# Sums of a masked attention spread over rows: broadcast and f32 transposes against two f32r parts and selector matmuls

## The chip, the cores and the metric

One core of one Trainium2 chip runs the whole program as one launch. The metric is the device time of one execution in microseconds (us); lower is better. TensorE is called PE below (its weight loads PEld), VectorE DVE, ScalarE ACT, GpSimd POOL, and SP is the engine that issues the DMAs.

## The reference, cut to what matters

Eight head pairs of attention (batch 2, 8 heads, 768 tokens, head size 64) with a mask from cluster numbers, and behind it two MLP layers (1536 tokens, 512 to 2048 to 512). Only the division by the sum of the exponentials bears on the change:

```python
    scores = scale * np.matmul(q, k.transpose(0, 1, 3, 2))
    scores = np.where(mask, scores, -1000000000.0)
    scores = scores - np.max(scores, axis=-1, keepdims=True)
    attn = np.exp(scores)
    attn = attn / (np.sum(attn, axis=-1, keepdims=True) + 1e-09)
    return np.matmul(attn, v).astype(np.float32)
```

## The kernel before, in words

The attention goes in 96 units of 128 query rows: 8 pairs (a batch and two heads), 2 heads, 3 groups of 256 rows, 2 tiles of 128. So a pair is 12 units. The kernel writes out the order of every engine's queue by hand (`tc.manual_schedule`, L340), in the loop at L985: in the round of unit u it issues the four score matmuls of u (`scores`, L714), the evacuation of a finished group (`drain`, L789), the exponentials of u-1 (`exps`, L730), the row maxima of u (`maxima`, L725), then the steps that are due in phase E of this round, then six f32 transposes of the exponentials of u-2 (`transposes`, L746), their split into two f32r parts by ACT (`highs`, L763) and DVE (`lows`, L767), then the 12 matmuls per group with the values in two halves (`attend`, L773), and last the steps due in phase L. A step due at a whole number x runs in phase L of round x, one due at x.5 in phase E of the next round (`at_`, L817, and L911).

PSUM is tight: `ps_s` has two tiles for scores, `ps_t` two for the transposes (so `pt` of unit u takes the tiles that DVE's `lows` of u-1 must have read), `ps_o` one for the sums of products, and `ps_m` one single bank, tag "m" (L203). That bank is taken in turn by the centroid dots (`dps`, L521), their transposes (`dt`, L548), the one-hot transposes (`ot`, L612) and the spread of the reciprocals (`rp_`, L861). The steps that prepare a later pair have due times in the table `STEADY` (L24): among them the dots at 5 to 7, `dt=10`, its last reader `dn=12.5` (DVE, L564: it multiplies `dt`), `ot0=20`, `ot1=21`. They count from 24 units ahead of that pair's first unit.

`finish(n)` (L820) divides pair n by its sums, with due times from `FINISH` (pairs 0 to 5), `FINISH_NEXT` (pair 6) and `FINISH_LAST` (pair 7), counted from the unit behind the pair's last one. POOL adds 1e-9 to the sums (`sg`, L835), DVE takes the reciprocals `rs` (128 rows x 6 tiles x 2 heads, L843), ACT copies them in two halves into `rx`, each reciprocal repeated over 64 columns (L851, 128x384 each). PE transposes `rx` by 128x128 pieces, three and three, into `rp_` (`spread`, L863), where a reciprocal then lies along the column of its query, repeated over the 64 rows of its head. DVE multiplies the products `xs` by it (`divide`, L872). Then ACT and POOL split `xs` into the MLP's f32r inputs `xh` and `xl` (L891, L903).

Behind unit 95 the MLP follows; its weights are converted from unit 82 on by ACT, DVE and POOL (`to_float32`, L154) between the attention's instructions.

Of the kernel before, what the change touches and what calls it, by code (L numbers as in the profile page):

```python
# [9 lines left out]
F32 = mybir.dt.float32  # L10
F32R = mybir.dt.float32r
# [3 lines left out]
ALU = mybir.AluOpType  # L15
# [32 lines left out]
]  # L48

FINISH = [3, 4, 7, 11, 14, 15, 16, 17, 19]  # L50
FINISH_NEXT = [3, 4, 5, 6, 7, 8, 9, 10, 14]
FINISH_LAST = [1, 1, 2, 3, 3, 3, 5, 5, 5]

MANUAL = 8
# [1 line left out]
P = 128  # L56
# [4 lines left out]
def kernel(  # L61
# [20 lines left out]
    nc = tc.nc  # L82
    B, NPAIR, _, _, S = qk_dim.shape
    H = 2 * NPAIR
    C = P // H
    D = P // 2
    NF, _, DM = w_out1.shape
    J = S // P
# [4 lines left out]
    HS = S // 2  # L93
# [10 lines left out]
    ident = const.tile([P, P], F32, name="ident")  # L104
    make_identity(nc, ident)
    identr = const.tile([P, P], F32R, name="identr")
# [96 lines left out]
    ps_m = ctx.enter_context(tc.tile_pool(name="ps_m", bufs=1, space=PSUM, reuse_waits="tile"))  # L203
# [114 lines left out]
    with ExitStack() as actx:  # L318
# [4 lines left out]
        ap4 = actx.enter_context(tc.tile_pool(name="ap4", bufs=1))  # L323
# [3 lines left out]
        def warm(n, pool=None):  # L327

            if pool is None:
                wps = ps_t.tile([P, 512], F32, tag="t", name="wps")  # L330
            else:
                wps = pool.tile([P, 2, 512], F32, tag="s", name="wps")[:, 0]
            for _ in range(n):
                nc.tensor.transpose(wps[:, 0:P], ident, ident)
# [71 lines left out]
            nc.vector.tensor_tensor(out=clz[:, :, mid], in0=csrc, in1=chz.bitcast(F32)[:, :, mid], op=ALU.subtract)  # L406

        todo = defaultdict(list)  # L410
        E, L = 0, 1
# [2 lines left out]
        def at(u, phase=L):  # L414
            def register(fn):
                todo[u, phase].append(fn)
            return register
# [7 lines left out]
        halves = [slice(t * HS, (t + 1) * HS) for t in range(2)]  # L425
# [391 lines left out]
        def at_(k):  # L817
            return at(int(-(-k // 1)), L if k % 1 == 0 else E)

        def finish(n):  # L820

            b, i = pairs[n]
            u0 = (n + 1) * UPP
            cuts = [slice(3 * t, 3 * t + 3) for t in range(2)]
            q = {}
            last = n == len(pairs) - 1
            ks = FINISH_LAST if last else FINISH_NEXT if n == len(pairs) - 2 else FINISH

            @at_(u0 + ks[0])
            def _():  # L830
                q["rs"] = ap4.tile([P, J, 2], F32, tag="rs", name="rs")
                q["sg"] = []
                for hh in range(2):
                    sg = ap4.tile([P, J], F32, tag="sg", name="sg", bufs=2)
                    nc.gpsimd.tensor_scalar(  # L835
                        out=sg, in0=sums.pop((n, hh)), scalar1=1e-9, scalar2=None, op0=ALU.add
                    )
                    q["sg"].append(sg)

            @at_(u0 + ks[1])  # L840
            def _():
                for hh in range(2):
                    nc.vector.reciprocal(out=q["rs"][:, :, hh], in_=q["sg"][hh])  # L843

            for t in range(2):

                @at_(u0 + ks[2 + t])
                def _(t=t):
                    if t == 0:
                        q["rx"] = ap4.tile([P, J, 2, D], F32, tag="rx", name="rx")  # L850
                    nc.scalar.copy(  # L851
                        out=q["rx"][:, cuts[t]], in_=q["rs"][:, cuts[t], :, None].to_broadcast([P, 3, 2, D])
                    )

            for t in range(2):

                def spread(t):
                    if last and t == 1:
                        rp_ = ps_t.tile([P, 512], F32, tag="t", name="rp_")
                    else:  # L860
                        rp_ = ps_m.tile([P, 512], F32, tag="m", name="rp_")  # L861
                    for j in range(3):
                        nc.tensor.transpose(  # L863
                            rp_[:, j * P : (j + 1) * P],
                            q["rx"][:, 3 * t + j].rearrange("p h d -> p (h d)"),
                            ident,
                        )
                    q["rp", t] = rp_

                def divide(t):  # L870
                    xs = xs_[n]
                    nc.vector.tensor_tensor(  # L872
                        out=xs[:, halves[t]], in0=xs[:, halves[t]], in1=q["rp", t][:, 0:HS], op=ALU.mult
                    )

                if last:
                    at_(u0 + ks[4 + t])(lambda t=t: spread(t))
                    at_(u0 + 4)(lambda t=t: divide(t))
                else:

                    @at_(u0 + ks[4 + t])
                    def _(t=t):
                        spread(t)
                        divide(t)

            where = slice(b * S, (b + 1) * S)
            for t in range(2):

                @at_(u0 + ks[6 + t])
                def _(t=t):  # L890
                    nc.scalar.copy(out=xh[:, i, where][:, halves[t]], in_=xs_[n][:, halves[t]])  # L891

            @at_(u0 + ks[8])
            def _():
                xs = xs_.pop(n)
                if last:
                    for eng, cut in zip((nc.vector, nc.gpsimd), halves):
                        eng.tensor_tensor(
                            out=xl[:, i, where][:, cut], in0=xs[:, cut],
                            in1=xh.bitcast(F32)[:, i, where][:, cut], op=ALU.subtract,  # L900
                        )
                    return
                nc.gpsimd.tensor_tensor(  # L903
                    out=xl[:, i, where], in0=xs, in1=xh.bitcast(F32)[:, i, where], op=ALU.subtract
                )
# [6 lines left out]
        for n in range(len(pairs)):  # L912
            finish(n)
        for entry in PRELUDE:
# [11 lines left out]
            else:  # L926
                steps[int(n[0])][name]()
        at(1)(lambda: warm(8))
        drains = []
        keys = [(n, hh, g) for n in range(len(pairs)) for hh in range(2) for g in range(NQ)]  # L930

# [17 lines left out]
        for F in range(2):  # L949
            todo[NU - 14, L].append(lambda F=F: begin(F))  # L950
            for j in range(2):
                start = NU - 12 + (0, 3, 6, 9)[2 * F + j]
# [685 lines left out]
```

## Time and profile before

| | us |
|---|---|
| median of 3 runs | 781.37 (781.03 to 781.65) |
| the profiled execution, its time | 782.5 |
| the profiled execution, its span from first to last instruction | 780.7 |
| mean granted TensorE clock in it, as a share of full speed | 0.996 |

A row of the timeline has the start and the length in us, the engine, the line of the kernel, the operation, the tiles it writes and reads, and in brackets the idle time of the engine ahead of it with what ended it; "x6" stands for six instructions merged. The chain of waits gives the work that ended last, followed back from the end: there the pieces of one engine follow each other without a gap, so that a piece's length is the time that its instructions really took on the path.

### The profile page before, as it was taken

How to read it: one execution, taken by the hardware profiler on the slowest of the kernel's cores; microseconds unless marked ns; L12 is line 12 of the kernel's file. 1: busy time of each engine (PE TensorE's matmuls, PEld its weight loads, DVE VectorE, ACT ScalarE, POOL GpSimd, SP SyncE). 2: the span in 40 equal slices, each digit the busy share in tenths (PEclk: the TensorE clock that was granted, in tenths of full speed). 3: DMA queues.
4: the chain of work that ended last, by engine and by line, in shares of the span. 5: the costliest groups of instructions: out<-in, count | busy, mean ns of one | idle time of the engine just before them, and what ended most of it. 6: DMA issues, size and time to landing. Idle time of an engine off the chain costs nothing.

```text
span 780.7 us, 12017 instructions
## 1 busy us (share of the span) xinstructions
PE 760.1 (97%) x4073; PEld 651.5 (83%) x4073; DVE 650.6 (83%) x1015; ACT 552.2 (71%) x1130; POOL 507.9 (65%) x510
## 2 busy tenths in 40 slices
PE   7699999999999899999999999999999999999998
PEld 6598999999999788788888888887888888888887
DVE  6778889889899767489967768799989898998965
ACT  5788999999899878365766766856965555655530
POOL 5666677886643545478758778598785766756810
PEclk9999999999999999999999999999999999999999
DMA  9857467566452350012112121211220302212004
GB/s 248 217 147 194 126 179 183 143 158 163 101 132 81 106 182 34 0 55 82 37 72 81 55 81 60 76 54 33 103 80 29 108 27 81 82 54 82 1 0 162
DMA packets 27101, 75.92 MB, mean 97 GB/s; under 512 B 4480, under 2 KB 7680, under 8 KB 27040
## 3 DMA queue, kind: packets, MB, share of 16 engines
q1 hardware_dynamic: 27040, 75.16, 32.9%
q8 instruction: 32, 0.52, 0.3%
q14 instruction: 29, 0.24, 0.1%
HBM read 49.36 MB, written 3.15 MB: 67 GB/s over the span
## 4 chain that ended last, share of the span: by engine, by line
PE 81%; ACT 6%; POOL 4%; DVE 3%; issue 3%; DMA 2%; SPq 0%; POOLq 0%; ACTq 0%; DVEq 0%
PE acc L1310 26%; PE hp L1146 9%; PE x L1146 8%; PE pt L749 7%; PE o L779 7%; PE v L1146 4%; PE acc L287 4%; PE s L721 4%; PE s L722 4%; PE hp L235 3%; PE z L1146 2%; DMA tok<-in_qk_tok_dram 1%; PE dps L525 1%; POOL sq L470 1%; ACT e L736 1%
## 5 line engine op out<-in xcount | busy, mean ns | idle before, releaser
L727 DVE TENSOR_REDUCE nm<-s 128x1 f32<-128x768 f32 x96 | 91.1, 949 | 17.4 <-PE s L722 17.2
L769 DVE TENSOR_TENSOR pl<-pt,ph 128x384 fp32r<-128x384 f32 x192 | 97.6, 550 | 8.3 <-ACT ph L765 7.6
L765 ACT CAST ph<-pt 128x384 fp32r<-128x384 f32 x192 | 84.1, 488 | 15.4 <-PE pt L749 14.7
L736 ACT ACTIVATE e<-s,nm 128x768 f32<-128x768 f32 x96 | 88.2, 918 | 3.4 <-DVE nm L727 2.9
L749 PE MATMUL pt<-ident,e 128*128 128x128 f32 x576 | 83.6, 278 | 6.0 <-DVE pl L769 6.0
L749 PEld LDWEIGHTS pt<-ident,e 128*128 128x128 f32 x576 | 67.4, 142 | 18.5 <-DVE pl L769 15.0
L1326 DVE TENSOR_TENSOR y<-y,acc 128x512 f32<-128x512 f32 x97 | 65.9, 680 | 15.9 <-PE acc L1310 15.6
L1333 POOL TENSOR_TENSOR y<-y,n 128x512 f32<-128x512 f32 x42 | 57.0, 1362 | 32.2 <-ACT n L1323 32.2
L1310 PE MATMUL acc<-oh,gl 128*128 128x512 f32 x190 | 74.0, 389 | 0.0
L1310 PE MATMUL acc<-oh,gh 128*128 128x512 f32 x190 | 74.0, 389 | 0.0
L1310 PE MATMUL acc<-ol,gh 128*128 128x512 f32 x190 | 74.0, 389 | 0.0
L175 DVE SCALAR_TENSOR_TENSOR r<-raw,r 128x512 uint32<-128x512 uint32 x64 | 65.6, 1025 | 4.0 <-issue 3.1
L721 PE MATMUL s<-ak,aq 128*128 128x384 f32 x192 | 68.9, 359 | 0.0
L722 PE MATMUL s<-mk,mq 80*128 80x384 f32 x192 | 65.7, 342 | 2.5 <-DVE mk L633 2.5
L182 POOL TENSOR_TENSOR tw<-m,r 128x512 uint32<-128x512 uint32 x26 | 34.0, 1308 | 48.4 <-DVE r L175 47.4
L187 POOL TENSOR_TENSOR il<-tw,ih 128x512 fp32r<-128x512 f32 x26 | 34.3, 1320 | 34.0 <-ACT ih L186 34.0
L182 POOL TENSOR_TENSOR t<-m,r 128x512 uint32<-128x512 uint32 x38 | 50.1, 1318 | 9.1 <-DVE r L175 9.1
L187 POOL TENSOR_TENSOR ol<-t,oh 128x512 fp32r<-128x512 f32 x32 | 46.8, 1461 | 11.6 <-ACT oh L186 11.6
L170 DVE TENSOR_SCALAR m<-m 128x512 f32<-128x512 f32 x64 | 47.5, 742 | 3.9 <-ACT m L166 3.8
L1146 PE MATMUL hp<-xl,ih 128*128 128x512 f32 x120 | 46.9, 391 | 1.4 <-DVE xl L1365 1.4
L1310 PE MATMUL acc<-gl,oh 128*128 128x512 f32 x120 | 46.8, 390 | 0.0
L1146 PE MATMUL hp<-xh,il 128*128 128x512 f32 x120 | 46.7, 390 | 0.0
(295 smaller groups left out, 2357.7 us busy)
## 6 DMA issues: line engine op xcount, KB each, us to landing
raw<-in_w_in_dram SPq DMA_DIRECT2D x32, 512.0 KB, 3.2
raw<-in_w_out_dram SPq DMA_DIRECT2D x32, 512.0 KB, 3.3
tok<-in_qk_tok_dram SPq DMA_DIRECT2D x8, 768.0 KB, 6.0
ak<-hi SPq DMA_DIRECT2D x31, 192.0 KB, 3.0
dim<-in_qk_dim_dram SPq DMA_DIRECT2D x6, 768.0 KB, 5.7
aq<-hi SPq DMA_DIRECT2D x16, 192.0 KB, 3.6
aq<-lo SPq DMA_DIRECT2D x16, 192.0 KB, 4.0
rawv<-in_v_dram SPq DMA_DIRECT2D x8, 384.0 KB, 4.0
```

The source lines that it names most:

```text
L182: nc.gpsimd.tensor_tensor(out=t.bitcast(U32), in0=mu, in1=r, op=ALU.add)
L187: nc.gpsimd.tensor_tensor(out=low, in0=t, in1=high.bitcast(F32), op=ALU.subtract)
L721: nc.tensor.matmul(s[:, c, 0:HS], lhsT=aq[:, qs], rhs=ak[:, ks], start=True, stop=False)
L722: nc.tensor.matmul(s[:, c, 0:HS], lhsT=mq[:, qs], rhs=mk[:, ks], start=False, stop=True)
L727: nc.vector.tensor_reduce(out=nm, in_=st[u]["s"][:, :, 0:HS], axis=AX.XY, op=ALU.max, negate=True)
L736: nc.scalar.activation(out=e.rearrange("p (a j) c -> p a (j c)", a=2), in_=st[u]["s"][:, :, 0:HS], func=AF.Exp, bias=st[u]["nm"], scale=1. ...
L749: nc.tensor.transpose(pt[:, j * P : (j + 1) * P], st[u]["e"][:, 3 * a + j, :], ident)
L765: nc.scalar.copy(out=dh, in_=src)
L769: nc.vector.tensor_tensor(out=dl, in0=src, in1=dh.bitcast(F32), op=ALU.subtract)
L1146: nc.tensor.matmul(o, lhsT=x_, rhs=y_, start=start and j == 0 and n == 0, stop=stop and j == len(ah) - 1 and n == 2, skip_group_check=chain,)
L1310: nc.tensor.matmul(acc, lhsT=a_, rhs=b_, start=s_ == 0 and n == 0, stop=s_ == 1 and n == 2)
L1326: nc.vector.tensor_tensor(out=y, in0=y, in1=acc, op=ALU.add)
```

## The change

For pairs 0 to 6 the reciprocals are no longer repeated by ACT and transposed whole. POOL splits `rs` into two f32r parts, 12 columns of high parts and 12 of low ones (`parts`, 128x24). One f32r transpose puts them into the bank of `ps_m` as 24 rows x 128 columns; ACT copies that to `rt`. `spread` then makes each 128x128 piece of `rp_` by a matmul of 24 rows: the stationary operand is a constant `sel`, which is 1 where the row is the high or the low part of the wanted reciprocal, and the moving operand is `rt`. `sel` is made once by POOL in round 11, in the buffer of `rx`. The new due times: `parts` at the due time of the reciprocals plus 0.5, the transpose at 13 and ACT's copy at 13.5 (pair 6: 5 and 5.5), where the two copies of ACT had 7 and 11 (pair 6: 5 and 6). `spread` and `divide` keep theirs (14 and 15; pair 6: 7 and 8). Pair 7 stays as it was.

```diff
--- before.py
+++ after.py
@@ -47,8 +47,8 @@
     "lt 1",
 ]
 
-FINISH = [3, 4, 7, 11, 14, 15, 16, 17, 19]
-FINISH_NEXT = [3, 4, 5, 6, 7, 8, 9, 10, 14]
+FINISH = [3, 4, 13, 13.5, 14, 15, 16, 17, 19]
+FINISH_NEXT = [3, 4, 5, 5.5, 7, 8, 9, 10, 14]
 FINISH_LAST = [1, 1, 2, 3, 3, 3, 5, 5, 5]
 
 MANUAL = 8
@@ -407,6 +407,14 @@
 
 
 
+        sel = ap4.tile([4 * J, 2 * J, D], F32R, tag="rx", name="sel")
+
+        def selectors():
+            both = ap4.tile([4 * J, 2 * J], F32, tag="rs", name="both")
+            eye = ident[0 : 4 * J]
+            nc.gpsimd.tensor_tensor(out=both, in0=eye[:, 0 : 2 * J], in1=eye[:, 2 * J : 4 * J], op=ALU.add)
+            nc.gpsimd.tensor_copy(out=sel, in_=both[:, :, None].to_broadcast([4 * J, 2 * J, D]))
+
         todo = defaultdict(list)
         E, L = 0, 1
         UPP = 2 * J
@@ -842,15 +850,40 @@
                 for hh in range(2):
                     nc.vector.reciprocal(out=q["rs"][:, :, hh], in_=q["sg"][hh])
 
-            for t in range(2):
-
-                @at_(u0 + ks[2 + t])
-                def _(t=t):
-                    if t == 0:
-                        q["rx"] = ap4.tile([P, J, 2, D], F32, tag="rx", name="rx")
-                    nc.scalar.copy(
-                        out=q["rx"][:, cuts[t]], in_=q["rs"][:, cuts[t], :, None].to_broadcast([P, 3, 2, D])
-                    )
+            def rows_of_sums():
+                q["rp"] = {}
+                ps = ps_m.tile([P, 512], F32R, tag="m", name="rt")
+                nc.tensor.transpose(ps[0 : 4 * J, 0:P], q["parts"], identr)
+                q["ps"] = ps
+
+            if last:
+                for t in range(2):
+
+                    @at_(u0 + ks[2 + t])
+                    def _(t=t):
+                        if t == 0:
+                            q["rx"] = ap4.tile([P, J, 2, D], F32, tag="rx", name="rx")
+                            q["rp"] = {}
+                        nc.scalar.copy(
+                            out=q["rx"][:, cuts[t]], in_=q["rs"][:, cuts[t], :, None].to_broadcast([P, 3, 2, D])
+                        )
+
+            else:
+
+                @at_(u0 + ks[1] + 0.5)
+                def _():
+                    q["parts"] = ap4.tile([P, 4 * J], F32R, tag="parts", name="parts")
+                    rs = q["rs"].rearrange("p j h -> p (j h)")
+                    high, low = q["parts"][:, 0 : 2 * J], q["parts"][:, 2 * J : 4 * J]
+                    nc.gpsimd.tensor_copy(out=high, in_=rs)
+                    nc.gpsimd.tensor_tensor(out=low, in0=rs, in1=high.bitcast(F32), op=ALU.subtract)
+
+                at_(u0 + ks[2])(rows_of_sums)
+
+                @at_(u0 + ks[3])
+                def _():
+                    q["rt"] = ap4.tile([4 * J, P], F32R, tag="rt", name="rt")
+                    nc.scalar.copy(out=q["rt"], in_=q["ps"].bitcast(F32)[0 : 4 * J, 0:P])
 
             for t in range(2):
 
@@ -860,17 +893,19 @@
                     else:
                         rp_ = ps_m.tile([P, 512], F32, tag="m", name="rp_")
                     for j in range(3):
-                        nc.tensor.transpose(
-                            rp_[:, j * P : (j + 1) * P],
-                            q["rx"][:, 3 * t + j].rearrange("p h d -> p (h d)"),
-                            ident,
-                        )
-                    q["rp", t] = rp_
+                        o = rp_[:, j * P : (j + 1) * P]
+                        if last:
+                            nc.tensor.transpose(o, q["rx"][:, 3 * t + j].rearrange("p h d -> p (h d)"), ident)
+                        else:
+                            k = 2 * (3 * t + j)
+                            pick = sel[:, k : k + 2].rearrange("p h d -> p (h d)")
+                            nc.tensor.matmul(o, lhsT=pick, rhs=q["rt"], start=True, stop=True)
+                    q["rp"][t] = rp_
 
                 def divide(t):
                     xs = xs_[n]
                     nc.vector.tensor_tensor(
-                        out=xs[:, halves[t]], in0=xs[:, halves[t]], in1=q["rp", t][:, 0:HS], op=ALU.mult
+                        out=xs[:, halves[t]], in0=xs[:, halves[t]], in1=q["rp"][t][:, 0:HS], op=ALU.mult
                     )
 
                 if last:
@@ -926,6 +961,7 @@
             else:
                 steps[int(n[0])][name]()
         at(1)(lambda: warm(8))
+        at(11)(selectors)
         drains = []
         keys = [(n, hh, g) for n in range(len(pairs)) for hh in range(2) for g in range(NQ)]
 
```

## Rows read from the trace of the kernel before

**Rows 1.** The page, busy time, share of the span, instructions.

```profile
PE 760.1 (97%) x4073; PEld 651.5 (83%) x4073; DVE 650.6 (83%) x1015; ACT 552.2 (71%) x1130; POOL 507.9 (65%) x510
```

**Rows 2.** Windows by stage: attention, its last 20 us, the rest; busy us, clock.

```profile
26.00:244.00 218.00, 213.27 (x1577) 197.92 (x1576) 194.82 (x340) 197.02 (x476) 144.64 (x183) 0.99 0.62 158
...
244.00:264.40 20.40, 17.50 (x124) 14.90 (x122) 18.30 (x35) 20.29 (x48) 8.75 (x10) 1.00 0.26 85
...
300.00:780.00 480.00, 475.92 (x2102) 393.28 (x2100) 395.49 (x569) 290.92 (x522) 319.70 (x254) 1.00 0.17 61
```

**Rows 3.** Waits of the weight loads in 60 to 244 us: total, times, longest.

```profile
PEld pt L749 <- DVE pl L769: 5.6, 25, 0.3
```

**Rows 4.** Chain of waits, long rounds of pairs 0, 1, 4: start us, us, what.

```profile
88.45 1.00 PE pt L749 x6
...
117.33 0.33 PE s L721
117.66 0.18 PE s L722
...
118.19 1.00 PE pt L749 x6
119.19 0.70 PE o L779 x6
119.90 0.18 PE s L721
...
120.61 0.99 PE pt L749 x6
121.60 0.71 PE o L779 x6
122.31 0.33 PE rp__1924 L863 x3
122.64 0.20 PE s L721
...
123.37 0.66 PE pt L749 x6
...
209.83 1.01 PE pt L749 x6
```

**Rows 5.** Timeline of rounds 36 to 38: ACT, DVE, POOL, weight loads.

```profile
115.51 0.50 ACT L851 COPY rx<-rs 128x384 f32<-128x384 f32 x1
...
116.17 0.90 ACT L736 ACTIVATE e<-s,nm 128x768 f32<-128x768 f32 x1
...
117.57 1.02 DVE L769 TENSOR_TENSOR pl<-pt,ph 128x384 fp32r<-128x384 f32 x2 [0.40 <-ACT ph L765]
...
117.89 0.21 POOL L141 TENSOR_SCALAR s<-s 128x24 f32<-128x24 f32 x1
...
118.18 0.31 PEld L749 LDWEIGHTS pt<-ident,e 128*128 128x128 f32 x3 [0.31 <-DVE pl L769]
...
118.51 0.29 DVE L142 RECIPROCAL rinv<-s 128x24 f32<-128x24 f32 x1
...
118.72 0.89 DVE L727 TENSOR_REDUCE nm<-s 128x1 f32<-128x768 f32 x1
...
119.53 0.54 DVE L564 TENSOR_TENSOR dn<-dt,rinv 128x384 f32<-128x384 f32 x1
119.99 1.01 DVE L769 TENSOR_TENSOR pl<-pt,ph 128x384 fp32r<-128x384 f32 x2
...
120.28 0.91 ACT L736 ACTIVATE e<-s,nm 128x768 f32<-128x768 f32 x1
```

**Rows 6.** Chain of waits, an f32r transpose with 64 stationary columns.

```profile
107.83 0.18 PE ot L614 x3
```

**Rows 7.** Groups by line of 60 to 244 us: busy us, mean ns.

```profile
L806 ACT COPY tmp<-o 128x256 f32<-128x256 f32 x37 | 13.9, 375 | 2.5 <-issue 1.6 <-POOL xs L813 0.4 <-PE o L779 0.3
...
L851 ACT COPY rx<-rs 128x384 f32<-128x384 f32 x12 | 6.1, 511 | 0.0
L686 POOL CAST vv<-rawv 128x384 fp32r<-128x384 f32 x12 | 6.0, 497 | 0.0
...
L835 POOL TENSOR_SCALAR sg<-sm 128x6 f32<-128x6 f32 x14 | 3.3, 236 | 1.1
```

**Rows 8.** Timeline of POOL, round 12, and round 89.

```profile
55.31 0.25 POOL L138 TENSOR_TENSOR s<-sq,s 128x24 f32<-128x24 f32 x1 [3.44 <-DVE s L137]
...
246.01 1.82 POOL L903 TENSOR_TENSOR xl<-xs,xh 128x768 fp32r<-128x768 f32 x1 [2.19 <-ACT xh L891]
```

**Rows 9.** Chain of waits, rounds 89 to 91.

```profile
245.88 0.20 ACT rx L851
...
248.77 0.41 ACT rx L851
249.18 0.89 ACT e L736 x2
```

## The prediction

> **What bounds the kernel now.** I read the page of the profile first: PE is busy for 97% of the span, DVE 83%, ACT 71%, POOL 65% [rows 1]. That is an average, so the windows by stage come next. From 300 us on PE has hardly a gap (475.92 of 480 us). In the attention PE (213.27 of 218), ACT (197.02) and DVE (194.82) all stand near full, and in its last 20 us the order turns round: ACT 20.29 of 20.40 us, PE only 17.50 [rows 2]. The change touches the attention alone, so the time hangs on two questions: where PE loses time before 244 us, and what ACT gets back behind it.
>
> The waits answer the first: the weight loads of the f32 transposes waited 25 times, 5.6 us in all, for DVE's `pl`, the split that frees the two banks of `ps_t` [rows 3]. The chain of waits places them. Six transposes take 0.66 us when nothing holds them, but 1.00 and 0.99 us in rounds 37 and 38, and the first score matmul of round 37 took 0.33 instead of 0.17 to 0.18 [rows 4]. Such long rounds come in twos, ten of them from 88.45 to 209.83 us, a couple for each of pairs 0 to 4 [rows 4]. The timeline tells why: ACT makes the second `rx` copy at 115.51, only then the exponentials (116.17) and the casts; DVE sits idle 0.40 us for the cast, its `pl` starts late at 117.57, and PE's loads wait 0.31 us for it [rows 5].
>
> **The change, part by part.**
>
> *PE, `spread`.* Six f32 transposes go, at 0.11 us each on the path (0.66 us for six, 0.33 for three) [rows 4]. Six f32r matmuls come, with 24 rows, 128 stationary and 128 moving columns, a form that the trace does not show. Below, it is bounded by the f32r transpose with 128 moving but only 64 stationary columns: 0.18 us for three, 0.06 each [rows 6]. Above, the nearest ordinary f32r matmul, 128 stationary and 256 moving columns, takes 0.71/6 = 0.12, and the one with 384 takes 0.18 [rows 4]. I take 0.11, the row with the same 128 by 128 shape: no gain, no loss. The loads of three such pieces took 0.31 us together [rows 5]. The Trainium skill (TensorE: Matmul & The Clock Gate, section on LDWEIGHTS) says that a load costs its columns and not its rows, so 24 rows save nothing; at its rate 128 columns are an estimated 107 ns, six 0.64 us. That speaks against a gain here, though the loads of [rows 5] came faster than that.
>
> *PE, the new transpose* of 128x24: one more f32r transpose, 0.06 us [rows 6], in each of seven pairs.
>
> *The new wait.* That transpose takes the one bank of `ps_m` at due time 13, phase L, so at the end of PE's round 37 (pair 1). Half a round earlier, in phase E of 37, stands DVE's `dn`, the last reader of the former tile `dt`. Before, the first to want the bank was `spread`, a round later. Behind the waiting transpose in PE's queue stand the scores of round 38, and behind those DVE's maxima and ACT's exponentials. Its size: before, `dn` ran from 119.53 to 120.07, PE's products ended at 119.90 [rows 4, 5]. In the changed kernel both move, see the sum. This clash is there for pairs 0 to 4; pairs 5 and 6 have no later pair being prepared.
>
> *ACT.* Two copies of 0.511 us go, one of 24x128 from PSUM comes. Between the copy of 256 columns (0.375) and of 384 (0.511) lie 0.136 us [rows 7]; one step further down gives an estimated 0.24. Net -0.78 us of ACT per pair. The first copy had no wait of PE near it and is worth nothing; the second is the one in [rows 5]. The new copy stands behind the exponentials of 37 (120.28 to 121.19 before [rows 5]) and ahead of the casts of 36; it ends by 121.4, and `spread` wants it only behind the products, near 121.9.
>
> *POOL.* Two operations on 128x12 per pair, 0.24 us each by the 128x6 row [rows 7]; `sel` is a sum of 24x12 and a copy of 768 columns, about twice the 0.497 us of 384 [rows 7], once. Cost nothing: `sel` stands in round 11, ahead of a POOL idle time of 3.44 us, and pair 6's parts ahead of one of 2.19 us [rows 8]. If that cover were gone, `sel` would push `rinv` of pair 2 by 1.2 us at most. SP's queue is not touched.
>
> *The sum.* Pair 1, in the times of [rows 4, 5]. With the copy of 115.51 gone, the score matmul of 117.33 loses its extra 0.15, the casts and `pl` come 0.4 us earlier (117.17), and the transposes run 118.04 to 118.70, the products to 119.40. DVE: the reciprocal `rinv`, which waits for POOL's row of 117.89, near 118.15, maxima at 118.36, `dn` 119.17 to 119.71. So PE waits 119.40 to 119.76 for the bank (0.36 us), transposes, and starts the scores of 38 at 119.82 against 119.90. By then `pl` (119.63 to 120.64) is ahead, so 0.71 of scores, 0.66 of transposes, 0.71 of products and 0.33 of `spread` follow without a gap: 122.23 against 122.64. Gain 0.41 us per pair: most of the 0.82 that PE lost, less what the new wait takes back. Five pairs: 2.05. Pair 5 has no such wait and pays 0.06. Pair 6 lies where ACT is the bound: the two `rx` copies hold 0.20 and 0.41 us of the chain [rows 9], in full slots 0.41 each, less 0.2 for the new copy, 0.6 at most; DVE is nearly full right behind, so I take 0.4 and keep 0 to 0.6. Sum -2.05 + 0.06 - 0.40 = -2.4 us. Against the profiled execution (782.5, of which 780.7 are the span) that is 780.1; that execution was 1.1 above the median of the runs, so the forecast for the median is 781.4 - 2.4 = 779.0.
>
> **The rivals.**
>
> *The stalls stay (781, same).* If DVE is late by its own work, two reciprocals, `dn` and `mx`, and not by ACT, the first wait remains: products end at 119.90, `dn` at 120.07, scores of 38 at 120.18. Then they no longer wait for `pl`, and `spread` ends at 122.59, a gain of 0.05. For: DVE runs without a gap from 118.51 [rows 5]. Against: its 0.40 us idle right before, ended by ACT [rows 5]. 5 x 0.05 + 0.34 = 0.6: 780.8.
>
> *Cheaper matmuls (777 to 778).* At 0.06 each the 36 of pairs 0 to 5 give 1.8 us more: 777.2. For: f32r moves columns at twice the rate of f32 [rows 4, 6]; against: 128 stationary columns must be loaded for only 128 moving ones.
>
> *Slower: narrow f32r products fall back to several passes.* Every f32r product of this kernel has 256 or more moving columns; only transposes have 128. If one of 128 took four passes, 4 x 0.06 = 0.24, `spread` would grow by 6 x 0.13 = 0.78 us. Then pairs 0 to 4 lose 0.37 each, pair 5 0.84, pair 6 still gains 0.4 (PE has room there): +2.3, 783.7. It decides from 0.176 us per matmul, where (0.176 - 0.11) x 36 eats the 2.4. For: no row of the trace has the form. Against: the time of the others follows their columns (0.12, 0.18). [...]
>
> **How the numbers follow.** Forecast 0.42 (about 778.4 to 780.2, with the new wait 0.2 us shorter or longer), stalls stay 0.2, cheaper 0.16, slower 0.22. A measurement of this kernel tells 0.2%, 1.6 us, from no change. Faster by more: 0.32 of the forecast's 0.42 and all 0.16, 0.48. Slower: most of the last rival, 0.2, and 0.02 of a wait for `dn` that is longer than worked out. Same: the remaining 0.30. The range takes in the cheap end and most of the slow one: 777.3 to 783.3.
>
> **What would show it.** Right: in the changed profile the six transposes near 118 and 121 us last 0.66 us in the chain, PE's idle time ahead of the new transpose is ended by DVE `dn` L564 at about 0.3 to 0.4 us for pairs 0 to 4, three selector matmuls hold 0.33 us, ACT is some 5 us less busy and PE's work nearly unchanged. Wrong: selector matmuls at over 0.17 us each; the waits for `pl` still there at 1.00 us; PE waiting at `spread` for ACT's copy; or a wait for `dn` of over 0.7 us, which would undo the gain.

## The result, and the profile after

The change made the kernel slower. Its median is 787.17 us (786.69 to 789.17) against 781.51 us for the kernel before in the same session, a ratio of 1.0071 with an interval of 1.0056 to 1.0085. The prediction was 779.0 us, its range 777.3 to 783.3, so the sign was wrong and the result lies outside the range. The profiled execution took 787.58 us, its span is 785.5 against 780.7.

The page says little. Its first part, to be read against [rows 1], has ACT less busy, by 3.0 us, and PE busier, by 5.4:

```profile
PE 765.5 (97%) x4080; PEld 655.5 (83%) x4080; DVE 653.6 (83%) x1015; ACT 549.2 (70%) x1123; POOL 511.2 (65%) x526
```

A clock made of like events says more. In the timeline I took the first `spread` of each pair and the distance to the next. In the kernel before they stand at 92.42, 122.15, 151.88, 181.63, 211.40, 238.02, 250.59 and 270.85 us; after, at 91.06, 121.72, 152.69, 183.56, 214.20, 241.66, 254.61 and 275.64. The four distances of steady work were 29.73 to 29.77 and are now 30.64 to 30.97, a mean of 30.79 against 29.75: 1.04 us per pair. The difference of the spans is made up like this: the start to pair 0's `spread` -1.36, four steady distances +4.16, to pair 5 +0.84, to pair 6 +0.38, to pair 7 +0.77, behind it 0.01; together +4.8. The start is no work of the change: over all runs below it varied from 90.5 to 93.7 us. The stage up to pair 7 goes with TensorE's granted clock. In after it is at half there (1.2 GHz) once, behind a stretch in which PE was busy for 11.67 of 13.30 us. A row has the window and its length, the busy us of PE, PEld, DVE, ACT and POOL, the granted clock, the share and GB/s of the DMA engines:

```profile
254.60:267.90 13.30, 11.67 (x81) 10.10 (x81) 12.30 (x24) 13.02 (x30) 4.74 (x5) 1.00 0.40 124
267.90:271.30 3.40, 3.04 (x16) 2.75 (x15) 1.92 (x4) 2.03 (x5) 3.29 (x3) 0.51 0.00 0
```

Before, it stayed at full speed (2.4 GHz) there:

```profile
250.60:270.80 20.20, 17.53 (x120) 14.96 (x119) 16.82 (x35) 18.95 (x42) 10.14 (x10) 1.00 0.29 95
```

The four steady stages have no such stretch in any run. So the distance is the sharper measure, and the experiments are read by it.

Now the rows that answer to the prediction. The waits of PE in 60 to 244 us, as [rows 3] (total, times, longest):

```profile
PEld pt L757 <- DVE pl L777: 5.1, 17, 1.9
PEld rt L856 <- DVE dn L572: 2.4, 5, 0.5
PE rt L856 <- DVE dn L572: 1.3, 5, 0.3
```

The loads wait for `pl` 17 times where it was 25, and the new wait for `dn` came at all five places foretold. The chain of waits of after, from pair 2's `spread` to pair 3's, answers to [rows 4]:

```profile
152.75 0.47 PE rp__2447 L902 x3
153.23 0.38 PE s L729
153.60 0.18 PE s L730
...
155.50 0.47 PE rp__2484 L902 x3
155.98 0.38 PE s L729
...
160.16 0.71 PE o L787 x6
...
162.10 0.98 PE pt L757 x6
163.09 0.71 PE o L787 x6
...
180.73 0.47 DVE dn L572
181.20 0.04 issue
181.25 0.23 PE rt L856
181.48 0.25 PE s L729
```

Two things here were not in the forecast. Three selectors hold PE for 0.47 us, where three transposes held it for 0.33, and the first score matmul behind them takes 0.38 instead of 0.20 [rows 4]. And there is a new long round, transposes of 0.98 us at 162.10, in a stretch where the kernel before had none. The timeline of after shows what DVE and POOL did just ahead of it:

```profile
158.30 1.84 POOL L478 TENSOR_TENSOR sq<-sq 128x768 f32<-128x768 f32 x1
...
158.73 1.83 DVE L518 SCALAR_TENSOR_TENSOR lo<-dim,hi 128x384 fp32r<-128x384 f32 x1
160.48 0.24 DVE L851 RECIPROCAL rs<-sg 128x6 f32<-128x6 f32 x2
160.65 0.91 DVE L735 TENSOR_REDUCE nm<-s 128x1 f32<-128x768 f32 x1
```

and the same place in the timeline of before:

```profile
127.93 0.55 DVE L510 SCALAR_TENSOR_TENSOR lo<-dim,hi 128x384 fp32r<-128x384 f32 x1
128.06 2.12 POOL L470 TENSOR_TENSOR sq<-sq 128x768 f32<-128x768 f32 x1
```

Neither instruction was touched. Before, `lo` (the low part of q and k, two inputs in SBUF) started 0.13 us ahead of POOL's fold of the squares; `lo` took 0.55 us and the fold 2.12, which ended 1.70 us behind `lo`'s end. After, the fold starts first and takes 1.84, and `lo` takes 1.83 and ends 0.42 us behind the fold. So the rows look as if whichever of these two comes second is held until the first is done, and after, DVE's maxima and split wait behind the loser. The groups by line, 26 to 244 us, count it (instructions, busy us, mean ns). Before:

```profile
L510 DVE SCALAR_TENSOR_TENSOR lo<-dim,hi 128x384 fp32r<-128x384 f32 x12 | 7.7, 643 | 0.0
```

After:

```profile
L518 DVE SCALAR_TENSOR_TENSOR lo<-dim,hi 128x384 fp32r<-128x384 f32 x12 | 12.6, 1052 | 0.0
```

The Trainium skill (SBUF — State Buffer, section Who interferes with whom) has this: a DVE instruction with two SBUF inputs and a GpSimd one that reads SBUF share a port that the first to start keeps for its whole length; "Issue order, not op shape, decides who blocks". These rows agree (1.83 us where `lo` takes 0.55 ahead of the fold, 2.12 where the fold takes 1.84 ahead of `lo`).

### The profile page after: what moved, and what is told of

The parts are those of the page before. It is cut to its first block, busy times and chain, and to the rows that moved or that the text cites. A ratio compares the mean times of both kernels' runs of the same rounds, so it can differ in the third digit from the quotient of the medians.

```text
span 785.5 us, 12040 instructions
## 1 busy us (share of the span) xinstructions
PE 765.5 (97%) x4080; PEld 655.5 (83%) x4080; DVE 653.6 (83%) x1015; ACT 549.2 (70%) x1123; POOL 511.2 (65%) x526
## 4 chain that ended last, share of the span: by engine, by line
PE 80%; DVE 8%; ACT 5%; POOL 3%; issue 3%; DMA 1%; SPq 0%; POOLq 0%; DVEq 0%; ACTq 0%
PE acc L1346 26%; PE hp L1182 9%; PE x L1182 8%; PE pt L757 6%; PE o L787 6%; PE hp L235 4%; PE acc L287 4%; PE v L1182 4%; PE s L729 4%; PE s L730 3%; PE z L1182 2%; DVE nm L735 1%; PE dps L533 1%; DVE pl L777 1%; DVE lo L518 1%
## 5 line engine op out<-in xcount | busy, mean ns | idle before, releaser
L1182 PE MATMUL hp<-xh,ih 128*128 128x512 f32 x120 | 46.7, 389 | 0.0
```

The lines of the kernel that those rows point to most:

```text
L1182: nc.tensor.matmul(o, lhsT=x_, rhs=y_, start=start and j == 0 and n == 0, stop=stop and j == len(ah) - 1 and n == 2, skip_group_check=chain,)
```

## The experiments

Two candidates, then: the row count of the selectors (TensorE pays on the way from 128 rows to 24 and back) and the collision of `lo` with the fold. The prediction's own terms, ACT's relief and the wait for `dn`, had to be priced beside them. All runs in one table; the distance is the mean of the four steady ones, the ratio is against the kernel before.

| run | rows | transpose's bank | fold | distance | median, us | ratio (interval) |
|---|---|---|---|---|---|---|
| before | - | - | before's | 29.75 | 781.51 to 782.18 | 1 |
| after | 24 | own | before's | 30.79 | 787.17 | 1.0071 (1.0056 to 1.0085) |
| e1 | 128 | own | before's | 30.44 | 785.89 | 1.0044 (1.0026 to 1.0061) |
| e2 | 24 | `dt`'s | before's | 30.78 | 787.46 | 1.0072 (1.0045 to 1.01) |
| e3 | 128 | `dt`'s | before's | 29.65 | 780.90 | 0.9991 (0.9978 to 1.0004) |
| e4, before + copies on POOL | - | - | before's | 29.37 | 781.41 | 0.9988 (0.9967 to 1.0009) |
| e5 | 24 | own | later | 30.28 | 784.64 | 1.0029 (1.0016 to 1.0042) |
| e6 | 24 | `dt`'s | later | 30.07 | 785.31 | 1.0033 (1.002 to 1.0046) |
| e7 | 128 | `dt`'s | later | 29.49 | 780.62 | 0.9971 (0.9958 to 0.9983) |
| e8 | 64 | `dt`'s | before's | 30.73 | 786.26, one run | - |
| e9, before + fold first | - | - | earlier | 30.36 | 783.96 | 1.0029 (1.0015 to 1.0044) |
| e10 | 128 | own | later | 29.71 | 782.18 | 1.0006 (0.9996 to 1.0016) |
| e11 | 96 | `dt`'s | later | 29.52 | 781.96, one run | - |

### e1_rows128: selectors and transposed reciprocals padded with zeros to 128 rows

```diff
-        sel = ap4.tile([4 * J, 2 * J, D], F32R, tag="rx", name="sel")
+        sel = ap4.tile([P, 2 * J, D], F32R, tag="rx", name="sel")
+        rt_all = ap4.tile([P, P], F32R, tag="rt", name="rt")
...
-                    nc.scalar.copy(out=q["rt"], in_=q["ps"].bitcast(F32)[0 : 4 * J, 0:P])
+                    nc.scalar.copy(out=rt_all[0 : 4 * J], in_=q["ps"].bitcast(F32)[0 : 4 * J, 0:P])
```

> The changed kernel with selectors and rt of 128 rows in place of 24, the further rows zero (one memset of rt by POOL in round 11). Theory A, the row count: a change between operands of 24 rows and of 128 rows on PE costs time at both ends of a group, so here three selector matmuls take 0.33 us or less in the chain of waits in place of 0.47, and the score matmul behind them 0.2 in place of 0.38; 0.64 us less per pair, for pairs 0 to 5 3.8 us: about 783.4. Theory B, the width: f32r matmuls of 128 moving columns take more than one pass; then 0.47 and 0.38 stay and the time stays at 787.

Measured: three selectors are down to 0.28 us and the score behind them to 0.23, as Theory A had it, but its time (783.4) was missed, and the distance fell only from 30.79 to 30.44. The four distances are not alike: 29.52, then 30.69, 30.85 and 30.68. The timeline shows why. In the first stage `lo` and the fold start together and DVE wins; in the next, POOL is ahead by 0.05 us. DVE:

```profile
98.96 0.55 DVE L520 SCALAR_TENSOR_TENSOR lo<-dim,hi 128x384 fp32r<-128x384 f32 x1
...
128.41 2.21 DVE L520 SCALAR_TENSOR_TENSOR lo<-dim,hi 128x384 fp32r<-128x384 f32 x1
```

POOL, at the same two places:

```profile
98.96 2.24 POOL L480 TENSOR_TENSOR sq<-sq 128x768 f32<-128x768 f32 x1
...
128.36 1.84 POOL L480 TENSOR_TENSOR sq<-sq 128x768 f32<-128x768 f32 x1
```

One kernel with the collision won once and lost three times: 1.2 us between the two. `lo` loses 1.66 us here (2.21 less 0.55), and 1.28 in after, where it started later behind the fold.

### e2_same_bank: the transpose into free columns of `dt`'s bank, due 10, for pairs 0 to 4

```diff
-                ps = ps_m.tile([P, 512], F32R, tag="m", name="rt")
+                if n < 5:
+                    q["ps"] = dts[n + 3].bitcast(F32R)[:, HS:512]
...
-                at_(u0 + ks[2])(rows_of_sums)
+                at_(u0 + (10 if n < 5 else ks[2]))(rows_of_sums)
```

> The changed kernel with the new transpose of pairs 0 to 4 written into the free columns 384 to 511 of the bank that dt holds, right behind dt (due 10), and copied by ACT at 10.5; pairs 5 and 6 as changed. Theory A, the bank: the wait of the transpose for dn goes (0.43 us of weight load idle, a transpose of 0.23 us alone and 0.07 more in the score behind it), 0.5 us per pair: about 784.7. Theory B, DVE: DVE is late in rounds 37 and 38 whatever PE does; the wait comes back ahead of the transposes of the exponentials as a wait for pl, and the time falls by under 1 us, to 786.3 or more.

Measured: 30.78, no gain, as Theory B had it, though the wait for `dn` is gone from the list of waits. `lo` still loses, 2.02 to 2.04 us in all four steady stages, and what PE saves in one place it waits in the other: the last four rounds of a pair fall from 9.73 to 9.53 us, and the six that hold `lo` rise from 15.55 to 15.75. Taking away the foretold wait alone shows nothing while another one holds the same round.

### e3_both: the edits of e1 and e2 together

```diff
+        rt_all = ap4.tile([P, P], F32R, tag="rt", name="rt")
...
+                    q["ps"] = dts[n + 3].bitcast(F32R)[:, HS:512]
```

> Both edits together: 128 rows, and the new transpose in the bank of dt. If both first theories hold the effects add to 6.3 us: about 780.9, level with the kernel before or a little under it. If the width and DVE are the causes, 786 to 787.

Measured: 29.65 and 780.90 us. Alone, the two edits gave 0.35 and 0.00 per pair, together 1.14. That the expected 780.9 was met is luck: it added two effects which, run alone, had given 0.35 of 0.64 us and nothing. That more comes out than the parts give is what pointed to a third thing: here `lo` starts 0.16 us ahead of the fold again (125.64 and 125.80) and takes 0.55. The starts of `lo` and the fold in the timeline, us from pair 1's first `spread`, tell what each edit does:

| | before | after | e1 | e2 | e3 |
|---|---|---|---|---|---|
| `lo` | 5.78 | 6.06 | 5.77 | 6.05 | 5.76 |
| fold | 5.91 | 5.64 | 5.72 | 5.83 | 5.92 |

With 24 rows in place of 128 `lo` comes 0.29 us later and the fold 0.08 to 0.09 earlier (e2 against e3, after against e1). With the transpose in a bank of its own the fold comes 0.19 to 0.20 earlier (e1 against e3, after against e2). Each of the two alone was enough to turn the order.

A smaller collision is left in e3. From the second stage on, the other `lo` of the pair starts 0.01 to 0.02 us behind POOL's `oh` and takes 0.90. In the timelines of POOL and DVE:

```profile
132.22 1.17 POOL L615 TENSOR_SCALAR oh<-dn 128x384 fp32r<-128x384 f32 x1
...
132.24 0.90 DVE L521 SCALAR_TENSOR_TENSOR lo<-dim,hi 128x384 fp32r<-128x384 f32 x1
```

The chain runs through it, and these stages take 29.75 or 29.76 us. The first, in which both start together and this `lo` takes 0.55, takes 29.34.

### e4_pool_copies: the kernel before, with `rx` of pairs 0 to 6 copied by POOL

```diff
-                    nc.scalar.copy(
+                    (nc.scalar.copy if last else nc.gpsimd.tensor_copy)(
```

> The kernel before with one edit: the two copies of the reciprocals of pairs 0 to 6 are made by POOL and not by ACT; transposes and banks as before. This prices the relief of ACT alone. Theory A, the prediction's step: 0.41 us per pair for pairs 0 to 4 or more (no new wait is added, so up to 0.8) and 0.4 for pair 6, so 2.4 to 4.4 us: 777 to 779. Theory B: the long rounds are DVE's own doing, ACT's relief is worth nothing: 781 to 781.5.

Measured: 29.37, so ACT's relief by itself is worth 0.37 us per pair; the total hides it (0.9967 to 1.0009). Its ten executions go from 778.22 to 784.22 us and go with the mean granted clock: three at 0.998 took 778.22 to 779.27 (two of the kernel before at 0.998 in the same session took 780.65 and 781.17), three at 0.987 to 0.989 took 783.26 to 784.22. In the profiled run the start was 0.94 us longer, pair 6's stage 0.25 and the stage up to pair 7, again with a stretch at half the clock, 0.67. In pair 6's stage DVE's `r` took 1.23 us beside POOL's `xs` and one of its new copies, and 0.69 before. The chain shows what is left of the two long rounds in front of `spread`:

```profile
148.34 0.74 PE pt L749 x6
149.09 0.72 PE o L779 x6
...
150.54 1.01 PE pt L749 x6
151.56 0.48 PE o L779 x4
```

The first long one has gone from 1.00 to 0.74, the second stays at 1.01 with no copy of ACT near it.

### e5_fold_later: the changed kernel, fold one step later (pairs 3 to 6)

```diff
-    sq0=0, hik0=1, hik1=2, lok=2, hiq0=3, hiq1=3, sq1=3, lt=3.5, fold0=4, lq0=4, dk0=4, dq0=5, de0=5.5,
+    sq0=0, hik0=1, hik1=2, lok=2, hiq0=3, hiq1=3, sq1=3, lt=3.5, fold0=5, lq0=4, dk0=4, dq0=5, de0=5.5,
```

> The changed kernel with one due time moved: POOL's first fold of the squares (sq, 1.84 us) in pairs 3 to 6 is placed one step later, behind the split of the reciprocals on the same queue, which cannot start before DVE has gone past its lo of that round. Nothing on TensorE changes. Theory of the collision (POOL's fold, started just before DVE's lo, holds lo off): lo is back at 0.55 us in those rounds where it took 1.83, and the distance from one pair's spread to the next goes from 30.9 us to 29.7 to 30.1, the time from 787.2 to 782.5 to 784. Rival (the narrow selectors and the transpose's wait on TensorE make the 1.04 us per pair by themselves): lo is short again, but the distance stays at 30.6 or more and the time at 786 to 788.

Measured: `lo` is at 0.55 us in every round of that kind, and the fold runs behind the split of the reciprocals. The timelines of DVE

```profile
157.32 0.55 DVE L518 SCALAR_TENSOR_TENSOR lo<-dim,hi 128x384 fp32r<-128x384 f32 x1
```

and of POOL:

```profile
158.64 1.84 POOL L478 TENSOR_TENSOR sq<-sq 128x768 f32<-128x768 f32 x1
```

The distance is 30.28, between what the two theories asked for: 0.51 of the 1.04 us was the collision, the rest was not. Neither theory was the whole.

### e6_bank_fold: later fold and `dt`'s bank, 24 rows

```diff
+    ... fold0=5, ...
+                    q["ps"] = dts[n + 3].bitcast(F32R)[:, HS:512]
```

> As the run with the later fold, and the transpose of the reciprocals of pairs 0 to 4 goes into free columns of the bank that holds dt's results, at an earlier point, as in the run with the shared bank; the selectors keep 24 rows. It prices the wait for a bank with the collision out of the way. Theory of the collision: the shared bank was worth nothing while lo was held off, and is worth the wait of 0.3 us per pair now: a distance of 29.5 to 29.8 us and 781.5 to 783.5 us. Rival (the bank is never what ends last): the same distance as the run with the later fold alone, within 0.1 us.

Measured: 30.07. The bank that gave 0.00 in e2 gives 0.21 with the collision out of the way, less than the theory asked for (0.3 in its words, 0.48 or more by its distance), and more than its rival's 0.1. The median of 785.31 is no better than e5's 784.64; the profiled run started 0.72 us later and lost 0.93 in the stage up to pair 7 (20.99 against 20.06), where the clock fell in it and not in e5.

### e7_all: 128 rows, `dt`'s bank, later fold

```diff
+    ... fold0=5, ...
+        rt_all = ap4.tile([P, P], F32R, tag="rt", name="rt")
+                    q["ps"] = dts[n + 3].bitcast(F32R)[:, HS:512]
```

> All three together: selectors and transposed reciprocals padded with zeros to 128 rows, the shared bank for pairs 0 to 4, the later fold. Theory: the run with 128 rows and the shared bank had already lost its collision (lo at 0.55 us, fold at 2.09 behind it) and stood at 29.75 us per pair; with the fold out of lo's way the pair distance is 29.4 to 29.75 and the time 779 to 781, no slower than before. Rival (the fold one step later delays work that waits for the norms): the distance grows to 30 or more and the time to 782 to 784.

Measured: 29.49 and 780.62 us, a ratio of 0.9971 (0.9958 to 0.9983): faster than the kernel before by 0.3%, and the best of the study. The chain at pair 2's `spread`:

```profile
150.17 0.28 PE rp__2443 L907 x3
150.46 0.23 PE s L732
150.69 0.18 PE s L733
```

### e8_rows64 and e11_rows96: at which count TensorE pays

```diff
-        sel = ap4.tile([P, 2 * J, D], F32R, tag="rx", name="sel")
+        sel = ap4.tile([64, 2 * J, D], F32R, tag="rx", name="sel")
```

(e3 with 64 rows; e11 is e7 with 96 in the same places.)

> The run with 128 rows and the shared bank, with 64 rows in place of 128 in the selectors and the transposed reciprocals. It asks whether the price of the selector matmuls goes with any row count other than 128, or only with a small one. If any change of the row count costs: three selectors in 0.40 to 0.47 us and the score matmul behind them at 0.37 to 0.38 us, as behind dt's 64 rows in the kernel before, and some 782 to 785 us. If only a count as small as 24 costs: 0.28 us and 0.23 us, as with 128 rows, and the time of that run, 781 us.

> All three edits, with 96 rows in place of 128. The score matmuls on mk and mq have 80 rows and stand beside those of 128 rows at the same 0.18 us without a longer one between them. If TensorE pays only where a count is at or under 64: three selectors in 0.28 us, the score behind them at 0.23, a distance of 29.5 us, as with 128. If it pays for any count that is not its neighbour's: 0.40 us or more, and 0.35 or more behind them, and 30.0 us.

Measured, in the chain of e8:

```profile
152.29 0.48 PE rp__2443 L907 x3
152.77 0.37 PE s L732
153.14 0.18 PE s L733
```

and in that of e11:

```profile
151.40 0.28 PE rp__2443 L907 x3
151.68 0.23 PE s L732
```

64 rows cost what 24 do, 96 what 128 do. The trace shows one more difference, the start of the first load of weights. Three loads take 0.41 or 0.42 us whatever the row count, but with 24 rows, in after, the first starts 0.01 us ahead of its product:

```profile
152.68 0.41 PEld L902 LDWEIGHTS rp__2447<-rt,sel 24*128 24x128 f32 x3
152.69 0.55 PE L902 MATMUL rp__2447<-rt,sel 24*128 24x128 f32 x3
```

and with 96, in e11, 0.11 us, beside the products in front of it:

```profile
151.12 0.42 PEld L907 LDWEIGHTS rp__2443<-rt,sel 96*128 96x128 f32 x3
151.23 0.45 PE L907 MATMUL rp__2443<-rt,sel 96*128 96x128 f32 x3
```

With 64 rows `lo` lost to the fold again (2.01 to 2.06 us, a distance of 30.73), so the time of e8, 786.26, lies above the 782 to 785 expected for that price. The moving columns, 128 of them, are the same in all of these, so their number is not what makes the difference.

### e9_fold_first_before: the collision alone, in the kernel before

```diff
-FINISH = [3, 4, 7, 11, 14, 15, 16, 17, 19]
+FINISH = [2.5, 4, 7, 11, 14, 15, 16, 17, 19]
...
+    ... fold0=3, ...
```

> The kernel before, with nothing of the change in it, and POOL's queue alone put in another order in the stages of steady work: the two additions to the sums (sg) go ahead of the squares, and the fold ahead of a partial sum (xs), so that the fold starts at about 0.8 us before DVE's lo of that round and not 0.1 us behind it. TensorE, DVE, ACT and the DMA queue keep their instructions and order. Theory of the collision: lo takes 1.4 to 1.8 us where it took 0.55, the round that waits for it is longer, the distance from spread to spread goes from 29.75 to 30.0 to 30.4 us and the time by 1 to 3 us, without a selector in the kernel. Rival (lo has slack, and only what TensorE gained in work was paid for): lo may be long, but the distance stays within 0.1 us of 29.75 and the time within 0.5 us.

Measured: `lo` takes 1.70 to 1.72 us behind the fold in all four steady stages, and the distance goes from 29.75 to 30.36, the time to 783.96. The timeline of POOL, pair 2's stage

```profile
157.86 1.84 POOL L470 TENSOR_TENSOR sq<-sq 128x768 f32<-128x768 f32 x1
```

and of DVE:

```profile
158.41 1.70 DVE L510 SCALAR_TENSOR_TENSOR lo<-dim,hi 128x384 fp32r<-128x384 f32 x1
```

There is no selector in this kernel, and TensorE, DVE and ACT have their old order. The fold was 0.55 us ahead of `lo`, not 0.8. So an order on POOL's queue alone is worth 0.61 us per pair.

### e10_rows_fold: 128 rows, later fold, own bank

```diff
+    ... fold0=5, ...
+        rt_all = ap4.tile([P, P], F32R, tag="rt", name="rt")
```

> The changed kernel with 128 rows in the selectors and the later fold, and the transpose in a bank of its own as the change has it. It is the one combination of the three edits that has not run. Theory: with 128 rows and no collision the distance was 29.52 us in the one stage of the run with 128 rows where lo was short, so it is 29.45 to 29.75 here and the time 780 to 782, whether or not the bank is shared; the shared bank then gives 0.0 to 0.2 us per pair. Rival (the wait for the bank costs the 0.36 us per pair that the prediction took): 29.85 or more and 782.5 or more.

Measured: 29.71, as the theory had it (the time, 782.18, lies just above its 782), and the bank is worth 0.22 at 128 rows (29.71 to 29.49), as at 24 (0.21). This run is the prediction with its two main blind spots taken away: selectors at the price of the old transposes, and no collision with the fold. It is 0.04 us per pair faster than before, and no faster in the median. It still pays something of its own: the other `lo` of the pair takes 0.61 us, and the last three dots, which need it, hold PE for 0.63 to 0.67 us instead of 0.53. In e1's one stage without either the distance was 29.52, a gain of 0.23.

## Why the prediction was wrong

The timeline gives the starts of the products of each round, and so the length of the rounds. From one pair's first `spread` to the next, in three parts (us, mean of the four steady stages):

| | two rounds with `spread` | six rounds | last four | sum |
|---|---|---|---|---|
| before | 4.82 | 15.08 | 9.85 | 29.75 |
| after | 5.50 | 15.55 | 9.73 | 30.78 |
| e4 | 4.81 | 15.05 | 9.51 | 29.37 |
| e5 | 5.50 | 15.04 | 9.74 | 30.28 |
| e6 | 5.50 | 15.04 | 9.53 | 30.07 |
| e7 | 4.83 | 15.14 | 9.52 | 29.49 |
| e10 | 4.82 | 15.15 | 9.74 | 29.71 |

Each column has one main cause: the first the selectors' rows, the second the collisions, the third ACT's relief and the wait for `dn`. In the third, one stage stands apart: from pair 2 to 3, after has 9.87 and e5 9.86, against 9.68 to 9.70 in the other three.

**PE, `spread`.** "I take 0.11, the row with the same 128 by 128 shape: no gain, no loss." This step failed, and is the largest: 0.69 us per pair in the first column, alike in the distance to pair 5, where DVE has no `lo` to make (27.46 after, 26.74 to 26.82 with 96 or 128 rows). The bound from above, 0.12 for one, was too low: it came from rows with 128 stationary rows and left the step from one count to another out. The sign set for it, over 0.17 us for one selector, did not show (0.47 for three is 0.157): more than half of the price stands in the score behind them, 0.38 instead of 0.20. The trace of before had shown that step, unread. Behind the transposes of `dt`, 64 rows, its chain has the score at twice its length:

```profile
142.19 0.52 PE dt L550 x6
142.71 0.37 PE s L721
```

The third rival had the sign and nearly the size, but another mechanism: f32r products of 128 moving columns are not slow by their width (0.28 us for three in e7 and e11, where four passes were put at 0.24 for one). The rival "Cheaper matmuls" had 0.06 for one, from a row with 64 stationary columns; with 128 it is 0.09, and the score behind takes 0.23 instead of 0.20, so next to nothing is gained.

**POOL.** "Cost nothing." It failed too: 0.51 us per pair. The new instructions on POOL show no cost of their own: `sel` took 0.81 us, POOL still stood idle for 2.45 us behind it, and no `parts` is in the chain from 84 to 260 us. But PE's longer rounds and its wait for `dn` delay `spread` and DVE, and not POOL, whose queue runs without a gap from its `dn` (151.79 in after, 0.90 us ahead of `spread` in the timeline; 151.27 before, 0.61 ahead) to the fold. Counted from the pair's first `spread` in the chain, `lo` started at 5.62 us before and at 5.98 after, the fold at 5.75 and 5.55. A lead of 0.13 us became a lag of 0.43. The text looked for who waits for the new instructions, not for which old ones would meet.

**ACT's relief and the new wait.** "Gain 0.41 us per pair: most of the 0.82 that PE lost, less what the new wait takes back." The wait was right in place and too large: 0.36 and a transpose of 0.06 were foretold, and the last four rounds are 0.21 shorter without both (9.74 in e5 and e10, 9.53 and 9.52 in e6 and e7), though the transpose itself, 0.23 us, and the score behind it, 0.25, take longer than foretold. The relief was sized more than double, 0.82. e4 gives it alone: 0.35 in that column, since of the two long rounds only the first goes; the second, 1.01 us, stays. So 0.12 is left of the two, 9.85 to 9.73, where 0.41 was forecast. The rival "The stalls stay" said that DVE would be late by its own work and that 0.05 per pair would be gained. That e10 gained 0.04 is near it by luck: it is 0.11 gained in the last four rounds, less 0.07 lost in the six. Of the signs, the transposes in front of `spread` did come at 0.66 us (151.39 in after's chain), and ACT is 3.0 us less busy, not 5. ACT's copy of `rt` took 0.238 us, where 0.24 was estimated.

**Pairs 5 and 6.** For pair 6 a gain of 0.4 was forecast. From pair 5's `spread` to pair 6's it was 12.57 us before and 12.95 after; with 96 or 128 rows it is 12.25 to 12.27 in four of five runs, a gain of 0.31, which the selectors' 0.70 turned round. e7 has 12.96 there: in its timeline ACT waits for a transfer of weights, and the chain of waits runs through that transfer.

```profile
236.89 0.68 ACT L166 ACTIVATE m<-raw 128x512 f32<-128x512 f32 x1 [0.95 <-DMA raw<-in_w_in_dram]
```

After has that wait too (0.94), but e2, e5, e6 and e8, with 24 or 64 rows, have 12.94 or 12.95 without it. The stage up to pair 7 goes by the granted clock: it took 19.98 to 20.26 us in the seven runs whose clock stayed at full speed there, and 20.64 to 21.06 in the six that have one stretch of some 3.4 us at half of it (after, e2, e3, e4, e6, e11). So the 0.77 us that after loses there are the clock's; e5, without such a stretch, has 20.06, 0.20 less than before. What made the clock fall in one run and not in another is open.

The sum per pair as it was, by the distances: +0.51 for the collision (after to e5), +0.57 for the rows (e5 to e10; their own column shows 0.69, and the six rounds give some of it back), -0.04 for what the prediction had counted (e10 to before; with the smaller loss in the six rounds). That is +1.04, where -0.41 was forecast. By the columns it is +0.69, +0.47 and -0.12. One detail of the text ahead of the prediction was off as well: the dots are due from 4 on, not from 5; nothing rested on it.

## What to carry to other kernels

A matmul over few rows between matmuls over 128 wasn't priced by its own shape here: look in the trace for the instruction behind the nearest one with 64 rows or fewer, and if it is long, try padding with zeros to over 64 (96 was enough here). An edit that shifts one engine by some tenths of a microsecond can turn the order in which DVE and POOL reach a shared resource; list the pairs that start within that shift (here 0.13 us), and put one behind the other by a dependence instead of by luck. Where runs differ by more than the edit is worth, measure between two like events inside the trace, over all stages and not one, and set the granted clock of the stretch beside it.

## What the hardware showed beyond that

- The row count: a group of three selectors and the score behind it took 0.47 + 0.38 us at 24 rows, 0.48 + 0.37 at 64, 0.28 + 0.23 at 96 and at 128; the scores with 80 rows stand among those of 128 at 0.18. The switch there and back is worth 0.34 us. The Trainium skill (TensorEngine Tiling (Array Packing), section Tiling Modes, Key Properties) says that a change of the tiling mode drains TensorE, and lists modes of 32, 64 and 128 rows. A line between 64 and 80 rows would fit that; no run here shows that the two are the same thing.
- The price of a collision depends on what else is late. Behind the fold `lo` cost 1.2 us per pair in e1, 0.61 in the kernel before and 0.51 in the changed kernel, and an edit that is worth 0.21 us gave nothing while it lasted (e2).
- A fall of the clock: a stretch of some 3.4 us at half of it, in the stage up to pair 7, goes with 0.65 us more (20.64 and 20.69 in e11 and e3, 19.99 and 20.04 in e10 and e7) to 0.97 (21.03 in after, 20.06 in e5).
